# A decode block's last weight matrix: 13 rows on every partition and two more on half of them, in place of 14 on all

## The chip, the cores and the metric

The kernel runs on one core of a Trainium2 chip. A core has engines that work side by side, each through its own list of instructions: TensorE (PE) multiplies matrices, VectorE (DVE) and ScalarE (ACT) work on rows of 128 partitions, GpSimd (POOL) does small jobs, and SyncE (SP) mostly issues transfers. Sixteen DMA engines move data between the chip's memory and the core's 128 partitions. Engines wait for each other, and for transfers, by semaphores.

The metric is the device time of one execution in microseconds (us). The kernel before was timed three times: 235.37, 235.56 and 235.78 us, with a median of 235.56. A further execution was taken with the hardware profiler, and the traces below are of that one.

## The reference, cut to what matters

One decode step of a transformer block for two sequences: a modulated attention over the last 4096 cached positions, then a feed-forward part with SiLU. All numbers are 32-bit floats.

```python
mod = (silu(c) @ w_mod).reshape(2, 6, 1, -1)
sa, ca, ga, sb, cb, gb = (mod[:, i] for i in range(6))
h = layernorm(x) * (1 + ca) + sa
x = x + ga * attention(h, k_cache, v_cache, wq, wo)   # 32 heads on 8 cached heads, width 128
h = layernorm(x) * (1 + cb) + sb
hid = silu(h @ w1)             # w1 is 512 x 1792
x = x + gb * (hid @ w2)        # w2 is 1792 x 512
```

## The kernel before, in words

With two tokens there is little arithmetic for each weight and each cached value, so the kernel reads nearly 98 MB once and computes beside the reading. Every call of an engine is recorded first (`Flow.record`, which finds what each operation needs), and `emit` then writes each engine's instructions in the order of the code. This order is the only scheduler. All instructions are emitted from one line of `emit`, so the profile gives them that one line, and one tells them apart by their tiles.

All large transfers are issued by SyncE, in the order of the code: `w_mod`, `wq`, the eight pieces each of `k_cache` and `v_cache`, `wo` in four pieces, `w1` in three, `w2` in five. They go into four slots of a large buffer, `store`. A transfer waits, before it is issued, until what stood in its slot has been read. `c` and `x` are loaded by two small transfers from ScalarE.

The end of the kernel is the feed-forward part. `hT_b` holds the normalised tokens, turned, with only two useful columns in each block of 32, and is the stationary operand of all products with `w1`. The 1792 columns of the hidden layer are cut into four groups of 448 (`FC`). The helper `product` puts group g on column group g of TensorE, so that four products run beside each other, into rows 32g to 32g+31 of one PSUM bank. There are four such rounds, one for each quarter k of the input; `fill` calls put idle matmuls between them. VectorE then turns the bank into `hidT` (128 partitions x 14 x 32), so that hidden column number 14p+t lies on partition p. From it come `z`, the SiLU by exponential (`sgh`) and `uT`.

`w2` is laid out to match: row 14p+t of the matrix lies on partition p at place t, so each partition holds 14 rows (`T2`) of 512 numbers, 2 KB a row. It is loaded in five transfers: rows 0 to 3, 4 to 7, 8 to 11, then 12 and 13 alone. Each of the first eight rows is one `product` of full width 512; the rows are shared over the four column groups, and the four partial sums are copied out (`copied`, on ScalarE, into `wide`) and folded into the output bank by four matmuls with `id4`. The rows from 8 (`WIDE`) on are multiplied by `narrow`, which cuts the 512 output columns into four quarters and adds straight to the output bank. After the last one VectorE multiplies by `gb` and adds `x1` (two operations into `yo`), and SyncE stores the result.

In the profile every recorded matmul call shows as two matmul instructions and two weight loads.

Of the kernel before, what the change touches and what calls it, by code (L numbers as in the profile page):

```python
# [9 lines left out]
P = 128  # L10
B, D = 2, 512
# [2 lines left out]
HP = HKV // 2  # L14
NP = HP * B
F = 1792
T2 = F // P
EPS = 1e-5
SLOT = 8192

# [112 lines left out]
def adaln_block(nc, x, k_cache, v_cache, wq, wo, w1, w2, c, w_mod, out):  # L133
# [7 lines left out]
    pe, dve, act, pool, sp = fl.pe, fl.dve, fl.act, fl.pool, fl.sp  # L141
# [6 lines left out]
    def buf(name, *shape):  # L148
        return nc.alloc_sbuf_tensor(name, list(shape), F32).ap()

    store = buf("store", P, 36864)
    slot = [store[:, i * SLOT : (i + 1) * SLOT] for i in range(4)]
# [6 lines left out]
    def bank(tag):  # L159
        banks[tag].append(banks[tag].pop(0))  # L160
        return banks[tag][-1]
# [3 lines left out]
    def const(shape, name):  # L165
        return buf(name, *shape)
# [95 lines left out]
    pool.memset(oTn, 0.0)  # L262
    mod_sp = const([P, 6, P], "mod_sp")
    x1 = const([P, P], "x1")
    hT, uT = const([P, 4, 32], "hT_b"), const([P, T2, 32], "uT")
    pool.memset(hT, 0.0)
    pool.memset(uT, 0.0)

    def silu_exp(t, name, shape):
        e = buf(name, *shape)  # L270
        dve.tensor_scalar(e, t, -1.0, 87.0, op0=ALU.mult, op1=ALU.min)
        act.activation(e, e, AF.Exp)
        dve.tensor_scalar(e, e, 1.0, None, op0=ALU.add)
        dve.reciprocal(e, e)
        return e
# [34 lines left out]
    sg = silu_exp(cT, "sgc", [P, 4, 32])  # L310
# [188 lines left out]
    def load_rows(w, per, lo, hi, s, at):  # L499
        e = w.shape[1]  # L500
        n = (hi - lo) * e
        sp.dma_start(s[:, at : at + n], w.rearrange("(p q) e -> p (q e)", q=per)[:, lo * e : hi * e])
        v = s[:, at : at + n].rearrange("p (q e) -> p q e", e=e)
        return {q: v[:, q - lo, :] for q in range(lo, hi)}

    wot, w1t, w2t = {}, {}, {}
    for lo, hi, s, at in ((0, 16, 2, 0), (16, 24, 3, 0), (24, 28, 3, 4096), (28, 32, 3, 6144)):
        wot |= load_rows(wo, 32, lo, hi, slot[s], at)
    for lo, hi in ((0, 2), (2, 3), (3, 4)):
        w1t |= load_rows(w1, 4, lo, hi, slot[0], lo * F)  # L510
    WIDE = 8
    for lo, hi in ((0, 4), (4, WIDE), (WIDE, 12), (12, 13), (13, 14)):
        w2t |= load_rows(w2, T2, lo, hi, slot[1], lo * D)

    gaT, sbT, cbT, xT = turned(ga, "gaT"), turned(sb, "sbT"), turned(cb1, "cbT"), turned(x_sp, "xT")
    dve.tensor_copy(hT[:, :, 1:32:16], sbT[:, :, 0:32:16])
# [30 lines left out]
    def fill(n):  # L547
        pe.matmul(
            bank("C")[:, :n], mean512, idle_w[:, :n], start=True, stop=True
        )  # L550

    def product(acc, w, rows, g, n, start, stop):
        pe.matmul(
            acc[32 * g : 32 * g + 32, :n], w, rows, start=start, stop=stop
        )

    def narrow(acc, w, rows, start, stop):
        for g in range(4):
            product(acc, w, rows[:, g * P : (g + 1) * P], g, P, start, stop)

    def copied(bank_):
        t = wide.pop()
        act.copy(t, bank_)
        return t
# [29 lines left out]
    dve.tensor_mul(sq, dT, dT)  # L594
    vs = buf("vs", P, B)
    dve.tensor_reduce(vs, sq.rearrange("p k b -> p b k"), axis=AX.X, op=ALU.add)
    FC = F // 4
    var = bank("B")
    pe.matmul(var[:, :B], mean512, vs, start=True, stop=True)
    std = buf("std_b", P, B)  # L600
# [1 line left out]
    rstd = buf("rstd_b", P, B)  # L602
    dve.reciprocal(rstd, std)
    fill(384)
    hp = bank("A")[:, :FC]
    for k in range(4):
        for g in range(4):
            product(hp, hT[:, k, :], w1t[k][:, g * FC : (g + 1) * FC], g, FC, k == 0, k == 3)
        if k == 2:
            fill(256)  # L610
    fill(512)
# [1 line left out]
    ax = buf("ax", P, P)  # L613
    dve.tensor_mul(ax, ao, ga)
    dve.tensor_add(x1, x_sp, ax)
    hidT = buf("hidT", P, T2, 32)
    dve.transpose(hidT, hp.rearrange("p (m t) -> p t m", t=T2))
    z = buf("z", P, T2, B)
    for b in range(B):
        dve.scalar_tensor_tensor(  # L620
            z[:, :, b],
# [3 lines left out]
            op0=ALU.mult,  # L625
            op1=ALU.add,
        )
    sg = silu_exp(z, "sgh", [P, T2, B])
    dve.tensor_mul(uT[:, :, 0:32:16], z, sg)
    yw = bank("D")  # L630
    for tt in range(WIDE):
        product(yw, uT[:, tt, :], w2t[tt], tt % 4, D, tt < 4, tt >= WIDE - 4)
    yw_sb = copied(yw)
    y = bank("D")[:, :P]
    narrow(y, id4, yw_sb, True, False)
    for tt in range(WIDE, T2):
        narrow(y, uT[:, tt, :], w2t[tt], False, tt == T2 - 1)
# [31 lines left out]
```

## Time and profile before

| | |
|---|---|
| median of three runs | 235.56 us (235.37 to 235.78) |
| the profiled execution: its own time | 235.64 us |
| the profiled execution: span from first to last instruction | 234.3 us |
| mean granted TensorE clock | 0.862 |
| busy: PE, DVE, ACT, POOL | 142.9, 113.9, 28.4, 8.1 us |
| moved | 97.68 MB, 417 GB/s on the mean of the span |

The span is 1.3 us shorter than the execution's time; the rest lies before the first instruction and behind the last. Busy times say which engine has work, not which engine is waited for: TensorE is busy for 61% of the span, but the transfers run at a nearly constant rate from start to end. The end of the kernel is read from the chain of waits, from the instructions in order of time, and from the share of the 16 DMA engines that are busy in short windows. In these a DMA share of 0.50 means that 8 of the 16 were busy on the mean.

### The profile page before, as it was taken

To read this page: it belongs to the slowest core of one execution; us is meant where nothing else is said; L and a number is where in the kernel's file an instruction comes from. 1 tells how busy PE (TensorE), PEld (TensorE's weight loads), DVE (VectorE), ACT (ScalarE), POOL (GpSimd) and SP (SyncE) were. 2 spreads that over 40 slices of the span, in tenths; PEclk is the share of its full clock that TensorE was granted. 3 is DMA by queue.
4 is the path that set the end of the run, shared out by engine and by line. 5 is a ranking of instruction groups with operands and counts; after the bars stand their busy time and mean duration, and the time that the engine had idled before them with its cause. 6 is when DMAs were issued, how large, how long until landed. Compare 5 with 4: busy or idle time off the path is not lost.

```text
span 234.3 us, 2365 instructions
## 1 busy us (share of the span) xinstructions
PE 142.9 (61%) x1024; PEld 38.4 (16%) x1024; DVE 113.9 (49%) x155; ACT 28.4 (12%) x63; POOL 8.1 (3%) x27
## 2 busy tenths in 40 slices
PE   0003963738275777856866855809774696497774
PEld 0001311100000202201201120200120122124212
DVE  4014100388596794694396377549349550201130
ACT  2003010000110401111100210210110032003201
POOL 4600000000000000000000000000000000000000
PEclk9999996776959977997667799985898779989999
DMA  7999999999999999999999999999999999999992
GB/s 268 445 423 425 431 422 448 442 436 414 431 421 448 439 420 431 425 428 431 442 436 420 422 442 431 436 432 425 422 442 431 425 428 431 414 413 426 419 416 95
DMA packets 4510, 97.68 MB, mean 417 GB/s; under 512 B 508, under 2 KB 532, under 8 KB 1044
## 3 DMA queue, kind: packets, MB, share of 16 engines
q1 hardware_dynamic: 4476, 97.52, 97.4%
q8 instruction: 8, 0.13, 0.2%
q14 instruction: 2, 0.02, 0.0%
q10 hardware_dynamic: 24, 0.01, 0.0%
HBM read 97.53 MB, written 0.00 MB: 416 GB/s over the span
## 4 chain that ended last, share of the span: by engine, by line
DMA 68%; DVE 23%; PE 6%; ACT 1%; issue 1%; POOL 0%; SPq 0%
DMA store<-in_A_k_cache_dram 25%; DVE kT L114 19%; DMA store<-in_A_wq_dram 16%; DMA store<-in_B_w_dram 14%; DMA store<-in_A_v_cache_dram 13%; PE bankD L114 4%; DVE store L114 2%; PE bankA L114 1%; ACT store L114 1%; PE bankB L114 1%; DVE wide L114 1%; DVE mx L114 1%; DVE qbd L114 0%; POOL qg L114 0%; PE bankC L114 0%
## 5 line engine op out<-in xcount | busy, mean ns | idle before, releaser
L114 DVE STREAM_TRANSPOSE kT<-store 128x2048 f32<-128x2048 f32 x32 | 71.1, 2279 | 17.8 <-DMA store<-in_A_k_cache_dram 17.8
L114 PE MATMUL bankA<-kT,qbd 128*32 128x512 f32 x256 | 47.7, 825 | 31.8 <-DVE kT L114 31.8
L114 PE MATMUL bankD<-store 128*32 128x512 f32 x256 | 36.2, 716 | 1.7 <-DMA store<-in_A_v_cache_dram 1.7
L114 PEld LDWEIGHTS bankA<-kT,qbd 128*32 128x32 f32 x256 | 5.7, 122 | 69.1 <-DVE kT L114 69.1
L114 PE MATMUL bankD<-store,hq_T 128*32 128x512 f32 x64 | 9.5, 746 | 5.9 <-DMA store<-in_A_wq_dram 5.9
L114 PEld LDWEIGHTS bankD<-store 128*32 128x32 f32 x256 | 8.8, 129 | 22.4 <-issue 20.1
L114 ACT COPY bias<-bankB 128x1 f32<-128x1 f32 x8 | 1.3, 159 | 89.4 <-PE bankB L114 89.4
L114 DVE STREAM_TRANSPOSE store<-store 128x512 f32<-128x512 f32 x8 | 5.7, 711 | 12.4 <-ACT store L114 12.4
L114 PE MATMUL bankB<-mv_a,avg 128*128 128x1 f32 x2 | 0.6, 362 | 16.7 <-DVE mv_a L114 16.7
L114 DVE TENSOR_REDUCE mx<-bankA 128x1 f32<-128x512 f32 x8 | 5.5, 692 | 10.7 <-PE bankA L114 10.7
L114 DVE TENSOR_TENSOR store<-store,half 128x512 f32<-128x512 f32 x16 | 10.3, 688 | 0.3
L114 DVE STREAM_TRANSPOSE wide<-bankD 128x512 f32<-128x512 f32 x2 | 1.4, 718 | 17.1 <-PE bankD L114 17.1
L114 PE MATMUL bankO<-store,pick 128*32 128x256 f32 x32 | 7.7, 382 | 2.9 <-ACT store L114 2.9
L114 PE MATMUL bankC<-store,sel 128*32 128x256 f32 x64 | 7.4, 414 | 3.1 <-DVE store L114 3.1
L114 ACT ACTIVATE store<-bankC,par 128x256 f32<-128x256 f32 x16 | 7.6, 476 | 10.9 <-PE bankC L114 10.7
L114 PE MATMUL bankD<-store,oTn 128*32 128x512 f32 x48 | 6.8, 729 | 3.4 <-DMA store<-in_A_wo_dram 3.4
L114 ACT COPY store<-bankD 128x512 f32<-128x512 f32 x8 | 4.7, 586 | 29.9 <-PE bankD L114 29.9
L114 PE MATMUL bankB<-ident,mx 128*1 128x128 f32 x16 | 3.1, 275 | 6.5 <-DVE mx L114 6.5
L114 PE MATMUL bankB<-negscale,mrow 1*128 1x1 f32 x16 | 3.7, 295 | 4.7 <-DVE mrow L114 4.7
L114 DVE STREAM_TRANSPOSE aoT<-bankA 128x128 f32<-128x128 f32 x1 | 0.3, 317 | 12.8 <-PE bankA L114 12.8
L114 DVE BATCH_NORM_STATS2 st_a<-x_sp 128x6 f32<-128x128 f32 x1 | 0.3, 295 | 12.4 <-DMA x_sp<-in_A_x_dram 12.4
L114 PE MATMUL bankA<-store,scT 128*32 128x256 f32 x32 | 3.6, 634 | 3.5 <-DVE scT L114 3.5
(117 smaller groups left out, 91.8 us busy)
## 6 DMA issues: line engine op xcount, KB each, us to landing
store<-in_A_k_cache_dram SPq DMA_DIRECT2D x8, 4096.0 KB, 29.9
store<-in_A_v_cache_dram SPq DMA_DIRECT2D x8, 4096.0 KB, 29.8
store<-in_A_wq_dram SPq DMA_DIRECT2D x2, 4096.0 KB, 31.9
store<-in_w_mod_dram SPq DMA_DIRECT2D x1, 6144.0 KB, 17.3
store<-in_A_wo_dram SPq DMA_DIRECT2D x1, 4096.0 KB, 31.9
store<-in_B_w_dram SPq DMA_DIRECT2D x3, 1024.0 KB, 31.1
store<-in_A_wo_dram SPq DMA_DIRECT2D x1, 2048.0 KB, 25.1
store<-in_A_wo_dram SPq DMA_DIRECT2D x2, 1024.0 KB, 28.2
```

The source lines that it names most:

```text
L114: ins = getattr(eng, method)(*args, **kw)
```

## The change

`w2` has 1792 rows. Its first 1664 (`FM`) are laid out as before, with 13 rows on each of the 128 partitions in place of 14, and loaded by four transfers (rows 0 to 3, 4 to 7, 8 to 11, 12). The last 128 rows go to partitions 0 to 63, two rows on each (`w2x`), by one transfer which is issued ahead of the four. Its source is written so that its outermost dimension has eight entries (`a`), each with eight runs of two rows: partition 8a+b gets rows 1664+16b+2a and the next one.

The products follow. The four groups of the hidden layer have 416 columns, and two further products per k, of 64 columns each, make the hidden values that belong to `w2x`, in a second PSUM bank; their columns are picked from `w1` so that they arrive on the partitions that hold the rows. VectorE turns this bank by a second transpose of 64 x 64. `hidT` is now allocated once and set to zero by GpSimd at the start, since half of its last two places is never written. `z`, `sgh` and `uT` have 15 places in place of 14. Two full-width products of 64 partitions (for `w2x`) stand ahead of the eight others, and one `narrow` is gone.

```diff
-T2 = F // P
+T2 = 13
+TX = 2
+HALF = P // 2
+FM = T2 * P
...
-    hT, uT = const([P, 4, 32], "hT_b"), const([P, T2, 32], "uT")
+    hT, uT = const([P, 4, 32], "hT_b"), const([P, T2 + TX, 32], "uT")
+    hidT = const([P, T2 + TX, 32], "hidT")
+    pool.memset(hidT, 0.0)
...
-    for lo, hi in ((0, 4), (4, WIDE), (WIDE, 12), (12, 13), (13, 14)):
-        w2t |= load_rows(w2, T2, lo, hi, slot[1], lo * D)
+    w2x = slot[1][:HALF, T2 * D : (T2 + TX) * D]
+    sp.dma_start(w2x, w2[FM:, :].rearrange("(b a t) e -> a b (t e)", a=8, t=TX))
+    for lo, hi in ((0, 4), (4, WIDE), (WIDE, 12), (12, 13)):
+        w2t |= load_rows(w2[:FM, :], T2, lo, hi, slot[1], lo * D)
...
-    FC = F // 4
+    FC = FM // 4
+    FX = (F - FM) // 2
...
-    hp = bank("A")[:, :FC]
+    hp, hx = bank("A")[:, :FC], bank("B")[:HALF, :FX]
     for k in range(4):
         for g in range(4):
             product(hp, hT[:, k, :], w1t[k][:, g * FC : (g + 1) * FC], g, FC, k == 0, k == 3)
+        extra = w1t[k][:, FM:].rearrange("p (b a t) -> p a b t", a=8, t=TX)
+        for g in range(2):
+            product(hx, hT[:, k, :], extra[:, 4 * g : 4 * g + 4], g, FX, k == 0, k == 3)
...
-    hidT = buf("hidT", P, T2, 32)
-    dve.transpose(hidT, hp.rearrange("p (m t) -> p t m", t=T2))
-    z = buf("z", P, T2, B)
+    dve.transpose(hidT[:, :T2, :], hp.rearrange("p (m t) -> p t m", t=T2))
+    dve.transpose(hidT[:HALF, T2:, :], hx.rearrange("p (m t) -> p t m", t=TX))
+    z = buf("z", P, T2 + TX, B)
...
+    for i in range(TX):
+        product(yw, uT[:HALF, T2 + i, :], w2x[:, i * D : (i + 1) * D], i, D, True, False)
     for tt in range(WIDE):
-        product(yw, uT[:, tt, :], w2t[tt], tt % 4, D, tt < 4, tt >= WIDE - 4)
+        product(yw, uT[:, tt, :], w2t[tt], tt % 4, D, TX <= tt < 4, tt >= WIDE - 4)
```

What stands on the engines at the end of the program follows, as built. In these rows the first name is what is written and the names behind the arrow are what is read; `store` holds the weights, and x8 counts the calls.

SyncE's transfers from the last piece of `wo` to the end, before (`in_B_w` are `w1` and then `w2`):

```order
L114 DMA store<-in_A_wo_dram 128x2048 x2
L114 DMA store<-in_B_w_dram 128x3584
L114 DMA store<-in_B_w_dram 128x1792 x2
L114 DMA store<-in_B_w_dram 128x2048 x3
L114 DMA store<-in_B_w_dram 128x512 x2
L114 DMA out_dram<-yo 4x2x128
```

And of the change:

```order
L117 DMA store<-in_A_wo_dram 128x2048 x2
L117 DMA store<-in_B_w_dram 128x3584
L117 DMA store<-in_B_w_dram 128x1792 x2
L117 DMA store<-in_B_w_dram 64x1x1024
L117 DMA store<-in_B_w_dram 128x2048 x3
L117 DMA store<-in_B_w_dram 128x512
L117 DMA out_dram<-yo 4x2x128
```

The transfer of 64 partitions is new and stands behind `w1` and ahead of the rest of `w2`; one of the two transfers of one row is gone.

TensorE from the last quarter of `w1` to the end, before (the name that ends in `dram` is missing here because weights are read from `store`; `bankC` takes the fills):

```order
L114 MATMUL bankA<-store,hT_b 32x448 x4
L114 MATMUL bankC<-qbd,mean 128x512
L114 MATMUL bankC<-qbd,mean 128x256
L114 MATMUL bankD<-store,uT 32x512 x8
L114 MATMUL bankD<-wide,id 32x128 x4
L114 MATMUL bankD<-store,uT 32x128 x24
```

And of the change:

```order
L117 MATMUL bankA<-store,hT_b 32x416 x4
L117 MATMUL bankB<-store,hT_b 32x64 x2
L117 MATMUL bankC<-qbd,mean 128x512
L117 MATMUL bankC<-qbd,mean 128x256
L117 MATMUL bankD<-store,uT 32x512 x10
L117 MATMUL bankD<-wide,id 32x128 x4
L117 MATMUL bankD<-store,uT 32x128 x20
```

Two matmul calls of 64 columns follow the four of `w1`, two calls of full width stand ahead of the eight of `w2`, and four of the 24 narrow calls are gone.

VectorE between the products with `w1` and those with `w2`, of the change (before, the second row was absent and the shapes were 128x448, 128x14 and 128x28):

```order
L117 STREAM_TRANSPOSE hidT<-bankA 128x416
L117 STREAM_TRANSPOSE hidT<-bankB 64x64
L117 SCALAR_TENSOR_TENSOR z<-hidT,rstd_b 128x15 x2
L117 TENSOR_SCALAR sgh<-z 128x30
L117 TENSOR_SCALAR sgh<-sgh 128x30
L117 RECIPROCAL sgh<-sgh 128x30
L117 TENSOR_TENSOR uT<-z,sgh 128x30
```

One instruction is added here, between the first transpose and `z`.

More of the change, by code (lines that the diff above doesn't have):

```diff
@@ L627, in adaln_block @@
         )
-    sg = silu_exp(z, "sgh", [P, T2, B])
+    sg = silu_exp(z, "sgh", [P, T2 + TX, B])
     dve.tensor_mul(uT[:, :, 0:32:16], z, sg)
     yw = bank("D")
+    for i in range(TX):
+        product(yw, uT[:HALF, T2 + i, :], w2x[:, i * D : (i + 1) * D], i, D, True, False)
     for tt in range(WIDE):
-        product(yw, uT[:, tt, :], w2t[tt], tt % 4, D, tt < 4, tt >= WIDE - 4)
+        product(yw, uT[:, tt, :], w2t[tt], tt % 4, D, TX <= tt < 4, tt >= WIDE - 4)
     yw_sb = copied(yw)
```

## The prediction, made before the result was known

> **What bounds the kernel now.** I read the page first, then the chain that ended last, then the last 12 us in order of time, then the DMA engines' share in short windows. The page (slices of the span, the queues, the chain's shares):
>
> ```profile
> DMA  7999999999999999999999999999999999999992
> q1 hardware_dynamic: 4476, 97.52, 97.4%
> q8 instruction: 8, 0.13, 0.2%
> q14 instruction: 2, 0.02, 0.0%
> q10 hardware_dynamic: 24, 0.01, 0.0%
> DMA 68%; DVE 23%; PE 6%; ACT 1%; issue 1%; POOL 0%; SPq 0%
> ```
>
> The DMA engines are full until the last slice, and 68% of the chain is transfers: the time is that of the stream, plus what comes behind its end. The chain's last pieces (start, length, what):
>
> ```profile
> 197.37 32.73 DMA store<-in_B_w_dram
> 230.10 0.04 issue
> 230.14 1.73 PE bankD L114 x48
> 231.89 0.30 DVE yo L114
> ...
> 232.22 0.29 DVE yo L114
> ```
>
> So rows 8 to 11 of `w2` land at 230.10 and release TensorE's narrow matmuls. The instructions there, in order of time (start, length, engine, operation; in brackets the idle time before and who ended it):
>
> ```profile
> 223.71 0.65 DVE L114 STREAM_TRANSPOSE hidT<-bankA 128x448 f32<-128x448 f32 x1 [5.04 <-PE bankA L114]
> ...
> 226.26 1.06 PE L114 MATMUL bankD<-store,uT 128*32 128x512 f32 x8 [1.13 <-DVE uT L114]
> ...
> 227.64 1.06 PE L114 MATMUL bankD<-store,uT 128*32 128x512 f32 x8 [0.32 <-DMA store<-in_B_w_dram]
> 228.77 0.59 ACT L114 COPY wide<-bankD 128x512 f32<-128x512 f32 x1 [3.39 <-PE bankD L114]
> ...
> 229.41 0.43 PE L114 MATMUL bankD<-wide,id 128*32 128x128 f32 x8 [0.71 <-ACT wide L114]
> 230.14 1.03 PEld L114 LDWEIGHTS bankD<-store,uT 128*32 128x32 f32 x40 [0.57 <-DMA store<-in_B_w_dram]
> 230.14 1.68 PE L114 MATMUL bankD<-store,uT 128*32 128x128 f32 x48 [0.30 <-DMA store<-in_B_w_dram]
> 231.40 0.16 PEld L114 LDWEIGHTS bankD<-store,uT 128*32 128x32 f32 x8 [0.23 <-DMA store<-in_B_w_dram]
> ...
> 232.54 0.70 SPq L114 DMA_DIRECT2D out_dram<-yo  x1
> ```
>
> The 40 weight loads of rows 8 to 12 issue in 1.03 us, to 231.17; the last row's eight start at 231.40, when it lands. So that landing costs about 0.2 us only, because TensorE is still working when it comes. The transfers' end, in windows (length, granted clock, DMA share, GB/s):
>
> ```profile
> 229.00:229.50 0.50, 1.00 0.63 242
> 229.50:230.00 0.50, 1.00 0.50 193
> 230.00:230.50 0.50, 1.00 0.44 168
> 230.50:231.00 0.50, 1.00 0.18 70
> ```
> ```profile
> 230.10:230.20 0.10, 1.00 0.53 205
> 230.20:230.30 0.10, 1.00 0.40 144
> 230.30:230.40 0.10, 1.00 0.27 102
> ...
> 230.90:231.00 0.10, 1.00 0.01 0
> ```
>
> The 16 engines don't end together. From 229.5 the share is 0.50: eight are done and eight late ones work on. The first late ones end at about 230.25 (0.53 falls to 0.40 and 0.27), the last at about 230.93. All 16 carry equal `w2` bytes, so lateness comes from elsewhere; the ten instruction fetches on the page, which go through the same engines, are the likely source.
>
> **The change, part by part.** *Bytes for each engine.* Between the landings that release 227.64 and 230.14 lies one load of 1024 KB, 64 KB an engine: 2.50 us, so 32 KB take 1.25 us and 16 KB 0.62. One row less on all partitions is 16 KB less for every engine. The new load has 256 KB; on eight engines it is 32 KB each. That it goes to eight is worked out from the queues: q10 held `c` and `x`, with four outer entries each, and its 24 packets are 2 x (8 data + 4), where the 4 are one closing packet for each engine used. On q1, 31 loads x (128 + 16) + 12 for the store give 4476: sixteen closing packets for loads of 128 partitions. Eight outer entries should make eight engines. In all, eight engines get 16 KB more and eight get 16 KB less.
>
> [...]
>
> *When the narrow matmuls start.* They wait for rows 8 to 11, not for the last row. An engine that doesn't carry the new load has the same bytes ahead of these rows as before, so this landing comes no sooner than 230.10. A loaded engine has 32 KB more ahead of it, 1.25 us. Early engines absorb it: they are done by 229.5, 1.4 us or more ahead of the last. A late one doesn't: one of the first late engines has 230.93 - 230.25 = 0.68 us of slack, so it would bring the landing 1.25 - 0.68 = 0.57 us later, to 230.67.
>
> *Narrow matmuls.* 40 in place of 48. The last starts 1.03 us behind the first and ends 0.28 later (mean 277 ns, next fence), 1.31 in all in place of 1.68, if row 12 lands within 0.9 us of the rows before it, which 0.62 us of transfer allows. That is -0.37 us.
>
> ```profile
> L114 PE MATMUL bankA<-store,hT_b 128*32 128x448 f32 x32 | 3.6, 548 | 1.0 <-DMA store<-in_B_w_dram 1.0
> L114 PE MATMUL bankD<-store,uT 128*32 128x512 f32 x16 | 2.1, 605 | 1.4 <-DVE uT L114 1.1 <-DMA store<-in_B_w_dram 0.3
> L114 PE MATMUL bankD<-store,uT 128*32 128x128 f32 x48 | 1.7, 277 | 0.3 <-DMA store<-in_B_w_dram 0.3
> ```
> ```profile
> 215.17 0.32 DVE L114 STREAM_TRANSPOSE aoT<-bankA 128x128 f32<-128x128 f32 x1 [12.79 <-PE bankA L114]
> 222.68 0.96 PE L114 MATMUL bankA<-store,hT_b 128*32 128x448 f32 x8 [0.59 <-DMA store<-in_B_w_dram]
> 224.39 0.52 DVE L114 SCALAR_TENSOR_TENSOR z<-hidT,rstd_b 128x14 f32<-128x14 f32 x2
> ```
>
> *Products with `w1`.* Eight matmuls last 0.96 us, of which one takes 0.55, so a round of four takes 0.41. With 416 columns two rounds shrink by 0.06; two more rounds of 64 columns add 0.82 x 64/448 = 0.12 by columns (bounds: nothing, if hidden behind the first transpose, to 0.82 at the price of a full round). I take +0.06. The earlier quarters lie under waits for `w1`.
>
> *VectorE.* The large transpose shrinks by 0.65 x 32/448 = 0.05. The new one of 64x64 isn't in the trace: below 0.32 (128x128), above nothing; I take 0.25 with its gap, near the 128x128. One more place in `z` and `sgh` is under 2% of 0.52 and its like. With the term above, partly hidden, `uT` comes 0.2 us later (bounds -0.1 and +1.1).
>
> *Wide products.* Two rounds last 1.06 - 0.605 = 0.45 plus the last matmul, so four products take 0.91. The two new ones use column groups 0 and 1, and the next four queue behind them: +0.91. Rows 4 to 7 then start at 226.26 + 0.2 + 0.91 + 0.91 = 228.28 in place of 227.64 (bounds 227.64, when it all hides, and 229.2). The copy and the `id4` matmuls follow 0.64 later, and the narrow ones could start at 229.41 + 0.24 + 0.64 = 230.29; the 0.24 is 8/40 of the 1.03 us plus a gap. Under a landing at 230.67 that is hidden; at 230.10 it costs 0.15.
>
> *GpSimd's memset* of `hidT` hides: GpSimd's memset of `uT`, of nearly its size, takes 0.47 us at 9.72, and 20 us of idle time follow.
>
> ```profile
> 9.72 0.47 POOL L114 MEMSET uT<- 128x448 f32 x1
> 30.31 0.53 POOL L114 TENSOR_SCALAR mod_sp<-mod_sp 128x128 f32<-128x128 f32 x1 [20.12 <-ACT mod_sp L114]
> ```
>
> **The sum**, with one late engine among the loaded eight: the narrow matmuls start at 230.67 + 0.04 = 230.71 and end at 232.02, in place of 230.14 + 1.68 = 231.82: +0.20. What follows is unchanged. The profiled execution took 235.64, so 235.84; it lay 0.08 above the median of the runs, so I forecast 235.76 for the median.
>
> [...]
>
> **Rivals.** *(A) All late engines are among the unloaded eight.* For it: eight are late, and the change unloads eight. Then the landing stays at 230.10, the narrow matmuls start at 230.29 and end at 231.60: -0.22, so 235.34 by the median. If the wide products hide, -0.37: 235.19. More can't be had, since TensorE needs 1.31 us from a landing that doesn't move.
>
> *(B) Slower: the last engines are among the loaded.* The landing moves by all of 1.25 us, to 231.35; the end moves by 1.25 - 0.37 = +0.88: 236.44. It decides from the point where a loaded engine has less than 1.25 - 0.37 = 0.88 us of slack: from there on the kernel is slower than before, by up to this price. [...]
>
> *(C) Writes into 64 partitions are slower.* If loaded engines get in each other's way and take 2.50 us instead of 1.25, even the early ones are late: the last early one ends at 229.5, and without the last two rows' 1.25 at 228.25. The last late one ends at 230.93 - 1.25 = 229.68, and the landing at 230.10 is 0.42 behind that, so 228.67 + 2.50 = 231.17, which is +0.70: 236.26; with the late one doubled too, up to 237.1. No transfer before writes 64 partitions, so no row speaks for or against.
>
> [...]
>
> *(D) The load is spread over all 16 engines.* Then each has 16 KB more ahead of rows 8 to 11, the landing comes 0.62 later, and the end moves by 0.62 - 0.37 = +0.25: 235.81.
>
> **How the numbers follow.** About 0.2%, or 0.47 us, is what a measurement of this kernel can tell from no change. The forecast has 0.42, (A) 0.28, (B) 0.08, (C) 0.15, (D) 0.07. The forecast, (D) and nearly all of (A) lie within 0.2%; (B) and most of (C) are slower. A gain over 0.47 lies beyond what (A) allows, but the run may differ from the profiled one, so it gets 0.11; slower 0.21; same 0.68. The range leaves out half of (B), the far part of (C) and the scatter below (A): 235.15 to 236.4.
>
> **What would show it.** In the profile of the changed kernel: the landing that releases the narrow matmuls, 0.57 us later against the end of `w1` (forecast), unmoved (A), over 1 us later (B, C). 40 narrow matmuls in 1.31 us without a wait inside. The DMA share of the last two microseconds: a fall without the plateau at 0.50 says that lateness was evened out. The wide products with rows 4 to 7 starting 0.6 us later, without a DMA wait. I am wrong if the late engines are others than I think, or if the new load is slower than 26 GB/s an engine.

## The result, and the profile after

The changed kernel takes 238.03 us in the median of four runs (237.81 to 238.17), the kernel before 235.56. The ratio is 1.0102, with a 95% interval of 1.0089 to 1.0114: slower by about 2.5 us, outside the range that was given.

The page of the changed kernel, queues and chain:

```profile
q1 hardware_dynamic: 4404, 97.52, 97.2%
...
DMA 66%; DVE 23%; PE 6%; SPq 2%; ACT 1%; issue 1%; POOL 0%
```

The bytes are those of before. The count of packets shows how the new load was dealt out: 30 loads x (128 + 16) + (64 + 8) + 12 = 4404, so it had eight closing packets and went to eight engines, as predicted. The chain's last pieces:

```profile
202.45 30.33 DMA store<-in_B_w_dram
232.78 0.04 issue
232.83 1.34 PE bankD L117 x40
...
234.52 0.29 DVE yo L117
```

Rows 8 to 11 of `w2` land at 232.78 in place of 230.10. The instructions in order of time:

```profile
224.20 0.91 PE L117 MATMUL bankA<-store,hT_b 128*32 128x416 f32 x8 [1.87 <-DMA store<-in_B_w_dram]
...
225.71 0.20 DVE L117 STREAM_TRANSPOSE hidT<-bankB 64x64 f32<-64x64 f32 x1
...
230.36 1.06 PE L117 MATMUL bankD<-store,uT 128*32 128x512 f32 x8 [0.48 <-DMA store<-in_B_w_dram]
...
232.83 1.30 PE L117 MATMUL bankD<-store,uT 128*32 128x128 f32 x40 [0.27 <-DMA store<-in_B_w_dram]
```

The narrow matmuls start 2.69 us later than before (232.83 against 230.14) and take 0.38 less (1.30 against 1.68). The sum, +2.31, is the growth of the span, from 234.3 to 236.6. So the whole loss lies in when that landing comes. And the delay does not begin there: the last quarter of `w1`, which stands ahead of the new load in the queue, already starts its products at 224.20 in place of 222.68.

What happened in between is plainest in the share and the rate of the DMA engines in one window of 6 us (length, granted clock, DMA share, GB/s; a packet counts in the window in which it starts, so a share can come out a little over 1). Of the kernel before:

```profile
220.00:226.00 6.00, 1.00 1.02 424
```

And of the changed kernel, the same window and three single microseconds in it:

```profile
220.00:226.00 6.00, 1.00 1.02 307
```
```profile
221.00:222.00 1.00, 1.00 1.07 258
222.00:223.00 1.00, 1.00 1.02 261
223.00:224.00 1.00, 1.00 1.01 229
```

The engines are as busy as before, but move 28% less: their packets take longer. At 6 x (424 - 307) = 702 KB this is 1.7 us of transfer. It isn't only the eight loaded engines that are slow. Eight at half speed and eight at full speed would move 318 GB/s, and here it is 229 to 261. The packet records of the kept trace, which no view prints, say it directly. The 114 packets of 2 KB and more that start between 221 and 224 us took from 412 to 684 ns for each 8 KB; in the kernel before, the 155 of the same stretch took from 309 to 324. Since all 16 engines are busy throughout, none kept its pace.

### The profile page after: what moved, and what is told of

Same layout as the page of the kernel before. It is cut to its first block, busy times and chain, and to the rows that moved or that the text cites. A ratio compares the mean times of both kernels' runs of the same rounds, so it can differ in the third digit from the quotient of the medians.

```text
span 236.6 us, 2391 instructions
## 1 busy us (share of the span) xinstructions
PE 138.7 (59%) x1036; PEld 37.8 (16%) x1036; DVE 114.0 (48%) x156; ACT 28.4 (12%) x63; POOL 8.6 (4%) x28
## 3 DMA queue, kind: packets, MB, share of 16 engines
q1 hardware_dynamic: 4404, 97.52, 97.2%
## 4 chain that ended last, share of the span: by engine, by line
DMA 66%; DVE 23%; PE 6%; SPq 2%; ACT 1%; issue 1%; POOL 0%
DMA store<-in_A_k_cache_dram 25%; DVE kT L117 19%; DMA store<-in_A_wq_dram 16%; DMA store<-in_B_w_dram 13%; DMA store<-in_A_v_cache_dram 13%; PE bankD L117 4%; SPq L117 2%; DVE store L117 2%; PE bankA L117 1%; ACT store L117 1%; PE bankB L117 1%; DVE wide L117 1%; DVE mx L117 1%; DVE qbd L117 0%; POOL qg L117 0%
## 5 line engine op out<-in xcount | busy, mean ns | idle before, releaser
L117 PE MATMUL bankA<-kT,qbd 128*32 128x512 f32 x256 | 49.4, 855 | 36.4 <-DVE kT L117 36.4
L117 PE MATMUL bankD<-store 128*32 128x512 f32 x256 | 29.1, 595 | 3.3 <-DMA store<-in_A_v_cache_dram 3.3
L117 PEld LDWEIGHTS bankD<-store 128*32 128x32 f32 x256 | 7.7, 109 | 18.1 <-issue 18.0
L117 PE MATMUL bankD<-store,oTn 128*32 128x512 f32 x48 | 8.2, 857 | 3.4 <-DMA store<-in_A_wo_dram 3.4
L117 PE MATMUL bankB<-negscale,mrow 1*128 1x1 f32 x16 | 3.0, 256 | 4.8 <-DVE mrow L117 4.8
```

Source lines behind the costliest of these rows:

```text
L117: ins = getattr(eng, method)(*args, **kw)
```

## The experiments

Three theories could be told apart. P: it matters which partitions an engine writes. S: it matters that eight engines read one small stretch of memory at once. U: any load on only half of the engines slows the rest. The row that begins with 220.00:226.00 is the window from 220 to 226 us of the kernel named. Of the code only the lines that matter are shown, and `...` stands for the rest; where the rows of `w2` change places, the columns of `w1` are picked to match.

**e1: another source, the same destination.** Two rows after every 26 of `w2` become the extra ones, so the reads are spread over the whole matrix. The loads of the other rows change with it: their source has 64 entries of two partitions each.

```diff
-    sp.dma_start(w2x, w2[FM:, :].rearrange("(b a t) e -> a b (t e)", a=8, t=TX))
+    rest = w2.rearrange("(b a s) e -> a b s e", a=8, b=8)[:, :, 2 * T2 :, :]
+    sp.dma_start(w2x, rest.rearrange("a b t e -> a b (t e)"))
...
```

> The two extra rows of w2 come from 64 places spread over the whole matrix (a pair after every 26 rows) in place of the last 256 KB of it; the transfer still has eight outer entries and writes the same partitions. Theory S (the slowness comes from where the new load reads, one small stretch of memory read by eight engines at once): the slow stretch goes, w1's last quarter lands as before, 235.3 to 236.0 us. Theory P (it comes from where it writes: engines write partitions that belong to another engine's way in): as slow as the changed kernel, 237.7 to 238.3 us. Theory U (any load on eight of sixteen engines slows the others): also 237.7 to 238.3.

Measured: 238.53 us (237.57 to 239.24), ratio 1.0122 (1.0090 to 1.0154).

```profile
220.00:226.00 6.00, 1.00 1.02 302
```
```profile
232.97 2.30 PE L117 MATMUL bankD<-store,uT 128*32 128x128 f32 x40 [0.27 <-DMA store<-in_B_w_dram]
```

The slow stretch is unchanged, and the narrow matmuls start at 232.97, as late as in the changed kernel (232.83). S is out. The median lies above the range that was written down. In the profiled execution, one of the two longer of the four, TensorE's granted clock is 0.55 in the microsecond from 233 and 0.50 from 234 to the end, and the 40 narrow matmuls take 2.30 us in place of 1.30.

**e2: the same source, another destination.** Two transfers of 32 partitions, so that run i of eight goes to four partitions in each, 4i to 4i+3 and 32+4i to 35+4i.

```diff
-    sp.dma_start(w2x, w2[FM:, :].rearrange("(b a t) e -> a b (t e)", a=8, t=TX))
+    for h in range(2):
+        sp.dma_start(
+            w2x[32 * h : 32 * h + 32, :],
+            w2[FM + 64 * h : FM + 64 * h + 64, :].rearrange("(b a t) e -> a b (t e)", a=8, t=TX),
+        )
...
-        extra = w1t[k][:, FM:].rearrange("p (b a t) -> p a b t", a=8, t=TX)
+        extra = w1t[k][:, FM:].rearrange("p (h b a t) -> p h a b t", h=2, a=8, t=TX)
```

> The source stays the last 256 KB of w2, but two transfers of 32 partitions take the place of the one of 64, so that run i of eight goes to partitions 4i to 4i+3 and 32+4i to 35+4i. Theory P: the slow stretch goes, 235.3 to 236.0 us. Theory S: as slow as the changed kernel, 237.7 to 238.3 us. Theory U: the same, 237.7 to 238.3.

Measured: 236.01 us in ten runs (235.63 to 236.21), ratio 1.0018 (1.0009 to 1.0028).

```profile
220.00:226.00 6.00, 1.00 1.02 422
```

The slow stretch is gone with two transfers on eight engines each (q1 has 4412 packets, 4404 - 72 + 2 x (32 + 8)), still ahead of the rest of `w2`, still from the same stretch of memory. P holds, and U is out. (That two transfers took the place of one is not the reason: d3 and d4 below have two as well, at 265 and 255 GB/s.) The median lies 0.01 above what P expected, and 0.42 above the kernel before. The trace of e2:

```profile
225.92 0.21 DVE L117 TENSOR_TENSOR uT<-z,sgh 128x30 f32<-128x30 f32 x1
...
226.18 2.04 PE L117 MATMUL bankD<-store,uT 64*32 64x512 f32 x12 [1.15 <-DVE uT L117]
...
228.45 1.06 PE L117 MATMUL bankD<-store,uT 128*32 128x512 f32 x8 [0.22 <-DMA store<-in_B_w_dram]
...
230.91 1.30 PE L117 MATMUL bankD<-store,uT 128*32 128x128 f32 x40 [0.27 <-DMA store<-in_B_w_dram]
```

The narrow matmuls start at 230.91, 0.77 later than before, and take 0.38 less: +0.39, near the 0.42 of the medians.

**e3: both edits.** Spread source and two transfers of 32 partitions, as in the code of e1 and e2.

> Both edits together: spread source and two transfers of 32 partitions. Theories S and P: 235.3 to 236.0 us, and if both share the blame this alone comes back in full while the two single edits come back in part. Theory U: 237.7 to 238.3 us.

Measured: 236.25 us (235.90 to 236.53), ratio 1.0028 (1.0016 to 1.0041), and the same rate as e2:

```profile
220.00:226.00 6.00, 0.90 1.02 422
```

It is a little above the range that was written down (up to 236.0). Spreading the source removes nothing of what e2 had left.

**e4: sixteen engines.** The 64 partitions are loaded from 64 row pairs in order.

```diff
-    sp.dma_start(w2x, w2[FM:, :].rearrange("(b a t) e -> a b (t e)", a=8, t=TX))
+    sp.dma_start(w2x, w2[FM:, :].rearrange("(p t) e -> p (t e)", t=TX))
...
```

> The load of 64 partitions has 64 outer entries in place of eight (row pairs in order), so that sixteen engines should carry it, 16 KB each. Theory P: two engines meet on each way in for a shorter stretch; some of the loss stays, 236.3 to 237.5 us. Theory S: the same 256 KB are read by sixteen engines in a short burst, 236.5 to 238 us. Theory U: the slow stretch goes, 235.6 to 236.1 us with the landing of rows 8 to 11 some 0.6 us later than before.

Measured: 237.17 us (237.07 to 237.91), ratio 1.0074 (1.0057 to 1.0091).

```profile
q1 hardware_dynamic: 4412, 97.52, 97.4%
```
```profile
220.00:226.00 6.00, 0.92 1.03 327
```

30 x 144 + (64 + 16) + 12 = 4412: sixteen engines carry it, and it is slow all the same, within what P expected. So the plainest way of loading 64 partitions costs too (327 GB/s); the eight runs of the change only cost more (307).

**d1 to d4: the load alone.** These four are the kernel before with 256 KB more to load, ahead of `w2` into columns that nothing uses; a GpSimd copy of one column waits for it. They compute all that the kernel before computes. They differ only in where run i of eight goes: d1 to 4i (and 32+4i), d2 to 8i, eight partitions long (by one transfer in place of two), d3 to 4i+4 (and 36+4i), d4 to 64+4i (and 96+4i).

```diff
+    for h, p0 in enumerate((0, 32)):          # d2: (0,) and 64 partitions; d3: (4, 36); d4: (64, 96)
+        sp.dma_start(
+            slot[1][p0 : p0 + 32, T2 * D :],
+            w2[1664 + h * 64 : 1664 + (h + 1) * 64, :].rearrange("(b a t) e -> a b (t e)", a=8, t=2),
+        )
...
+    pool.tensor_copy(const([P, 1], "sink"), slot[1][:, T2 * D : T2 * D + 1])
```

> The kernel before, computing as before, with 256 KB more to load ahead of w2 that nothing but a GpSimd copy of one column reads: eight engines, two transfers of 32 partitions, run i to partitions 4i to 4i+3 and 32+4i to 35+4i. This is the price of 32 KB more on eight engines alone. Theory P: packets as fast as others, rows 8 to 11 land 0.5 to 0.8 us later than before because late engines are among the loaded; the last row up to 1.25 us later; 236.1 to 236.8 us. If all late engines were unloaded: 235.5 to 235.7.

> The same 256 KB in one transfer of 64 partitions, run i of eight to partitions 8i to 8i+7, as in the changed kernel. Theory P: a stretch of some 4 us in which all packets take up to twice their time, as in the changed kernel; rows 8 to 11 land 2.5 to 3 us later than before; 238.0 to 238.9 us. If the slowness needed the changed layout of w2 or its products: as d1.

> As d1, but each run lies four partitions further: run i to partitions 4i+4 to 4i+7 (and 36+4i to 39+4i). No two of the eight engines write the same group of four at once when they run in step, but each writes the group that its neighbour has in d1. Theory P in the form 'each engine has a way in of its own, and a foreign one is shared with its owner': slower than d1 by some tenths to 2 us, packets up to twice as long while owner and guest overlap. In the form 'only two guests on one way collide': as d1.

> As d1, but on partitions 64 to 127: run i to 64+4i to 67+4i, then 96+4i to 99+4i. If the way in is one for a group of partitions and its counterpart 64 higher, as d1. If partitions 64 to 127 have ways of their own that belong to the other eight engines, each is shared by two engines for the length of the load: packets up to twice as long, 237 to 238.5 us.

Measured:

| | us | ratio to before (95%) | run i of eight goes to |
|---|---|---|---|
| d1 | 236.55 | 1.0051 (1.0032 to 1.0071) | 4i, 32+4i |
| d2 | 238.84 | 1.0151 (1.0113 to 1.0189) | 8i |
| d3 | 240.54 | 1.0217 (1.0191 to 1.0243) | 4i+4, 36+4i |
| d4 | 239.01 | 1.0166 (1.0132 to 1.0200) | 64+4i, 96+4i |

The windows, of d1:

```profile
220.00:226.00 6.00, 1.00 1.01 420
```

of d2:

```profile
220.00:226.00 6.00, 1.00 1.01 304
```

of d3:

```profile
220.00:226.00 6.00, 0.95 1.02 265
```

and of d4:

```profile
220.00:226.00 6.00, 0.91 1.02 255
```

The same bytes from the same place cost next to nothing in rate (d1: 420 against 424) or 39% of d1's rate (d4). Each transfer is carried by eight engines: d1, d3 and d4 have 4556 packets on q1, 4476 + 2 x (32 + 8), and d2 has 4548, 4476 + (64 + 8). That the two transfers of d1, d3 and d4 go to the same eight was taken for granted, and no row shows it. The place that is written decides. A shift by four partitions is enough (d3, 265 GB/s against d1's 420), although there no two of the eight runs write the same group of four partitions. So it doesn't take two of the runs on one group. What d1 to d4 show is this: with run i on the groups that it has in d1 the stream keeps its rate, and with run i on others it falls. Which engine carries which run no view and no record names. In d2, as in the change, runs 0 and 7 write a group that they have in d1 for half their length (0 to 3, and 60 to 63), and d2 is milder than d3 and d4 (304 GB/s against 265 and 255).

d3 and d4 came out above what was written down: d3 3.99 us above d1 where 2 at most was expected, d4 0.51 above its range. The times of d2 and d3 hold some of TensorE's clock besides (0.50 from 231 to 233 us in d2, and from 231 on in d3), so the rates carry the comparison there. d4 runs at full clock behind 222 us:

```profile
233.39 1.68 PE L114 MATMUL bankD<-store,uT 128*32 128x128 f32 x48 [0.31 <-DMA store<-in_B_w_dram]
```

Its narrow matmuls start 2.48 later than those of d1, which the next rows show, and its median is 2.46 higher.

d1 shows the other part, the price of the uneven load itself:

```profile
230.91 1.69 PE L114 MATMUL bankD<-store,uT 128*32 128x128 f32 x48 [0.27 <-DMA store<-in_B_w_dram]
...
232.17 0.16 PEld L114 LDWEIGHTS bankD<-store,uT 128*32 128x32 f32 x8 [0.23 <-DMA store<-in_B_w_dram]
```

With nothing changed but 256 KB more, 32 KB an engine if both transfers go to the same eight, and GpSimd's copy, rows 8 to 11 come 0.77 us later (230.91 against 230.14), exactly as in e2, and so does the last row (232.17 against 231.40).

**e6: the extra rows behind the rows that are waited for.** As e2, with the two transfers issued between rows 8 to 11 and row 12, and their products made narrow at that place.

```diff
+    for tt in range(WIDE, T2):
+        if tt == T2 - 1:
+            for i in range(TX):
+                narrow(y, uT[:HALF, T2 + i, :], w2x[:, i * D : (i + 1) * D], False, False)
+        narrow(y, uT[:, tt, :], w2t[tt], False, tt == T2 - 1)
```

> [...] If what is left over in e2 is the landing of rows 8 to 11, held up by late engines among the loaded eight: rows 8 to 11 land at about 230.1 again, the last row at about 231.5, as in e2, and the time lies between before and e2, 235.6 to 235.9 us. If the rest in e2 comes from the changed products and not from the loads: as e2 or slower, 236.0 us and over.

Measured: 235.82 us in eleven runs, ratio 1.0009 (1.0000 to 1.0018).

```profile
230.29 2.01 PE L117 MATMUL bankD<-store,uT 128*32 128x128 f32 x56 [0.23 <-DMA store<-in_B_w_dram]
231.87 0.16 PEld L117 LDWEIGHTS bankD<-store,uT 128*32 128x32 f32 x8 [0.20 <-DMA store<-in_B_w_dram]
```

The median is 0.22 above the kernel before in place of e2's 0.42, so about half of what e2 had lost is back, within the range that was written down. Rows 8 to 11 are back at about 230.25. Now the last row, at about 231.8 where 231.5 was expected, ends the last wait. The trace itself shows no gain over e2 (a span of 234.8 against 234.7): the profiled execution, at 236.14, is one of the two longest of the eleven. None of the versions is faster than the kernel before.

**f1: the kernel before with sixteen runs.** The five loads of `w2` take its rows in another order, from 16 outer entries of eight runs each; the columns of `w1` are picked to match. All 128 partitions are written, and no load is uneven.

```diff
-        w2t |= load_rows(w2, T2, lo, hi, slot[1], lo * D)
+        sp.dma_start(
+            slot[1][:, lo * D : hi * D],
+            w2.rearrange("(b a q) e -> a b (q e)", b=8, q=T2)[:, :, lo * D : hi * D],
+        )
...
```

> The kernel before, but all five loads of w2 take the matrix in another order of rows, so that their source has 16 outer entries of eight runs each (partition 8a+b gets the 14 rows from 14 x (16b+a)) in place of 128 equal steps; the columns of w1 are picked to match. If engine e then writes partitions 8e to 8e+7, as run e of eight did in the changed kernel: all packets of w2 slow, rows 8 to 11 land 4 to 8 us later, 240 to 244 us. If a load of 128 partitions is dealt out by partitions whatever its source: as before, 235.4 to 235.8 us.

Measured: 243.97 us (243.76 to 244.37), ratio 1.0357 (1.0343 to 1.0371).

```profile
220.00:226.00 6.00, 0.90 1.04 241
```
```profile
224.00:226.00 2.00, 1.00 1.02 233
...
230.00:232.00 2.00, 0.85 1.07 246
```
```profile
237.46 2.79 PE L114 MATMUL bankD<-store,uT 128*32 128x128 f32 x48 [0.65 <-DMA store<-in_B_w_dram]
```

Sixteen busy engines (4476 packets on q1, as before) move 229 to 246 GB/s as long as they load `w2` (windows of 2 us from 222 to 232). So the slowness needs neither half the partitions nor half the engines; a source cut into 16 runs of eight partitions is enough. Of the 8.4 us by which the span grows, 7.32 are the later start of the narrow matmuls (237.46 against 230.14), and 1.11 their length at a granted clock of 0.50 (2.79 against 1.68). By itself f1 doesn't part writing from reading, as e1 and d1 to d4 do, since the eight pieces of a run now lie 448 KB apart in `w2`.

A source of 64 runs of two partitions isn't slow: e1 and e3 load the other rows of `w2` in that way, and e3 keeps 422 GB/s. So it isn't the cutting of a source into runs alone. How such a source is dealt out to the engines the runs don't show.

Of the dealings that were tried, that of e2, e3 and d1 kept 422, 422 and 420 GB/s, and of the others (the change, e1, e4, d2, d3, d4, f1) none was over 327. How the plain loads of 128 partitions are dealt out to the engines no row shows; what is measured of them is their rate, 424 GB/s before.

## Why the prediction was wrong, step by step

- **The new load goes to eight engines**: right, by 4404 packets.
- **32 KB on a loaded engine take 1.25 us**: wrong, and this is the step that failed. The price was taken from loads of all 128 partitions in order. While the new load ran, the whole stream fell from 424 to between 229 and 261 GB/s. That is 14 to 16 GB/s an engine on the mean, below the 26 that the prediction named as the sign of being wrong, and the landing of rows 8 to 11 moved by 2.68 in place of 0.57. Why, e2 and d2 show: the same load, dealt to other partitions, costs none of this rate, and in the kernel before, with the change's dealing, it costs the same (304 GB/s against 307). So it matters which partitions the load writes.
- **Rival (C)** came nearest, with 0.15, and priced the change at 236.26, or up to 237.1 (237.0 by its own terms: 2.50 - 0.68 - 0.37 = 1.45 over 235.56). It was right that the writes of the loaded engines are slow. It was wrong that 64 partitions make them so: e2 and d1 write 64 at 422 and 420 GB/s, and f1 writes 128 at 241. And it let only the loaded engines slow down, by half. That 32 KB take 2.50 us on a loaded engine is a term that no run shows; what the runs showed is that all engines slow down (412 to 684 ns for 8 KB in place of 309 to 324), and `w1`'s last quarter, still in flight, slows with them (its products start 1.52 us later). Its price was 1.8 us too low. Nothing in the trace of before could price it, but that was a reason for a wider range.
- **A late engine among the loaded eight makes rows 8 to 11 late**: right in the landing. With the slow writes taken out, they come 0.77 us later (e2, d1), where 0.57 was forecast. That a late engine is among the loaded ones was the author's estimate, and no row or run names the engines; if it is so, at a price of 1.25, the late loaded engine had 0.48 us of slack and not 0.68. In e2 this gives +0.42 us in the median, where the forecast had +0.20. Rival (A), in which they don't move, is refuted by d1.
- **40 narrow matmuls in 1.31 us**: 1.30, without a wait inside.
- **The wide products could take rows 4 to 7 at 228.28**: in e2 TensorE waited 0.22 for them until 228.45, so it was ready at 228.23, and that is covered. But the agreement is luck in part: the wide products began at 226.18 in place of 226.46 (0.28 early) and lasted 2.04 in place of 1.82. And the sign "without a DMA wait" did not come true, since rows 4 to 7 came later too.
- **VectorE's second transpose, 0.25 with its gap**: 0.20, or 0.23 with its gap (225.71 to 225.94). GpSimd's memset cost nothing that shows.
- **Rival (D)**, sixteen engines, did not come about in the change; in e4 the rate fell too (327 GB/s).

The 2.31 us between the two profiled executions (2.47 between the medians) are so made up: the narrow matmuls start 0.77 later by the uneven load (e2 against before) and 1.92 later by the place of the writes (232.83 against e2's 230.91), and fewer of them gain 0.38.

## What to carry to other kernels

Before a load's source is cut into runs to steer it to some engines, work out which partitions each run will write: here only run i of eight on 4i to 4i+3 and 32+4i to 35+4i kept the rate (422 and 420 GB/s against 424), and the other dealings to 64 partitions moved 255 to 327. A busy DMA share with a falling rate (1.02 at 307 GB/s) is the sign that this went wrong. To take bytes off engines that end late, look at what is waited for last: the 256 KB more ahead of rows 8 to 11 made that landing 0.77 us later in d1, and in e2, where a whole row of 256 KB behind it was saved, it came just as late. What can't be priced from the trace, here a write of 64 partitions, is better tried first by itself, as a load that nothing uses, like d1 to d4.

## What the runs showed of the hardware that was not expected

- While the change's load of 256 KB on eight engines ran, the packets of all 16 engines were slow, those that don't carry it among them: a DMA share of 1.01 to 1.07 at 229 to 261 GB/s, and no packet of 2 KB and more from 221 to 224 us under 412 ns for 8 KB, where 309 to 324 was the pace before. The same bytes to other partitions left 420 GB/s (d1). Why the others slow down, too, isn't settled; reads from a crowded stretch are ruled out by e1 (302 GB/s).
- Another order of the source's rows, with all 128 partitions written, took the window from 220 to 226 us from 424 to 241 GB/s (f1). f1 is 3.6% slower, of which about an eighth is TensorE's clock in the narrow matmuls.
- The 16 engines, with equal bytes of `w2` by the count of packets, don't end together: before, the DMA share is 0.50 in the half microsecond from 229.5 us, 0.44 in the next and 0.18 in the one behind it. That instruction fetches cause this was argued in the prediction and not tried.
